# Attention, maxout and softplus layers in one kernel: turns of q a slot earlier, turns of k at the end of a batch

## The chip, the cores and the metric

The kernel runs on one core of one Trainium2 chip. The metric is the time of one execution on the device, in microseconds. TensorE does the matrix products, VectorE (DVE) and ScalarE (ACT) the work on elements, SyncE (SP) starts most of the transfers. What is measured is the median of several executions; the lines of a profile come from one profiled execution.

## The reference

The inputs are q, k, v of shape (8 batches, 8 heads, 576, 64), a short sequence p (8, 8, 32, 64), three weights of 512 x 768, one of 768 x 512, one of 512 x 2048 and one of 2048 x 512. Cut to what is computed:

```python
def sm_attn(qq, kk, vv):
    s = scale * np.matmul(qq, kk.transpose(0, 1, 3, 2))
    s = s - np.max(s, axis=-1, keepdims=True)
    a = np.exp(s)
    a = a / (np.sum(a, axis=-1, keepdims=True) + 1e-09)
    return np.matmul(a, vv)
p_packed = sm_attn(p, k, v)                  # 32 rows per head
out = sm_attn(q, p_packed, p_packed)         # 576 rows per head
x = out.transpose(0, 2, 1, 3).reshape(4608, 512)
h = np.maximum(np.maximum(x @ w1, x @ w2), x @ w3)   # layers 1
x = h @ w_out                                        # layer 2
h = x @ w_in                                         # layer 3
g = np.maximum(h, 0.0) + np.log1p(np.exp(-np.abs(h)))
y = g @ w_out2                                       # layer 4
```

The weights come as 64-bit numbers and the products are made to nearly full 32-bit precision.

## The kernel before

**Precision.** A product of two 32-bit matrices is made of three products: each operand is split into a part "hi" (`split`, ACT, L107) and a rest "lo" (DVE, L108), and hi x hi, hi x lo and lo x hi are added (`three`, L396). Names with hi and lo are such pairs: a2 (the attention weights of a batch), pw (the packed values times the first weights), h (the maxout), wi (weights of layer 3), x2 (its inputs).

**First stage, batch by batch.** A prelude with an order written out by hand does batch 0 and prepares batch 1. Then a loop over n = 1 to 7 does layer 1 and layer 2 of batch n, and between them, in small pieces, the attention of batch m = n + 1. A batch has ten slots. Slots 0 to 5 are the six blocks f of layer 1, three units w each (`layer1_unit`, unit u = 3 x slot + w). A unit is 24 matmuls; the first maxout copy `m` of a block is on ACT (L419), the two others are a maximum on DVE (L421). One slot later `layer1_split` splits the block into hhi (ACT) and hlo (DVE). Slots 6 to 9 are the four blocks e of layer 2, whose results xs leave ACT for the buffer x2d in device memory.

**The attention pieces** stand at fixed units: `attn1_scores` (p times k, needs all four turned pieces of k) at u = 5, its transposes at 9, the values at 13, `attn2_scores` (q times packed p, needs all four turned pieces of q) at 18, behind layer 1. `packed_weights`, which makes a part of pw (matmuls ps_w, L375), stands at u = 1, 5, 9, 13 and 18.

**Loads and turns.** q and k of a batch are loaded in four pieces each (`load_raw`, two heads a piece, four DMAs of 140 KB, L158, tiles qraw and kraw from one pool `rx` of four buffers). A piece is then turned, which is a transpose of 32 x 32 blocks on DVE (`transpose_kq`, L223 for k, L220 for q), into its part of the tile vT. vT has one buffer, for k and q by turns. Two lists, `loads` and `turns`, say in which slot a piece is loaded and turned, for which batch ahead.

**Narrowing.** The weights of layers 3 and 4 are 64-bit. In slots 0 to 5 `narrow_ahead` loads a block of them (L635), takes one that was loaded three steps before, makes it 32-bit with one ACT step (L79) and three DVE steps (L86, L89, L97) and stores it from the SP queue (L631, wi<-x).

**The last batch** has no attention to prepare. There the kernel loads the weights of layer 3 in 32 bits (`wi_x`, L684, four buffers), two per slot, and splits each one slot later (wihi on ACT, wilo on DVE). At the end of slot 5 it asks for the first four pieces of x2 (`x2r<-x2d`, L701), which are split in slots 7 and 8.

**What sets the order.** The pieces of TensorE's work are chained in the order of the program text (`pinned`). For DVE, ACT and SP the framework's scheduler chooses each engine's order, from the program text and its own model of when operands are there. Each engine and each queue runs its list in order, and each instruction waits for its operands.

**Second stage.** Layers 3 and 4 take 144 steps (`layer3` with the softplus, `layer4`, L782 to L784), after all batches.

Of the kernel before, what the change touches and what calls it, by code (L numbers as in the profile page):

```python
# [1 line left out]

# [17 lines left out]
def packed_attention_maxout_softplus(  # L20
# [22 lines left out]
    nc = tc.nc  # L43
# [5 lines left out]
    DF2 = wi2.shape[1] // 2  # L49
# [5 lines left out]
    KC = DM // P  # L55
    F1 = DF1 // P
# [49 lines left out]
    def split(src, hi, lo):  # L106
        nc.scalar.activation(out=hi, in_=src, func=AF.Copy)  # L107
        nc.vector.tensor_tensor(out=lo, in0=src, in1=hi.bitcast(F32), op=ALU.subtract)  # L108
# [10 lines left out]
    wsb_ctx = ExitStack()  # L119
    wsbp = wsb_ctx.enter_context(tc.tile_pool(name="wsbp", bufs=1))  # L120
    at_ctx = ExitStack()
    rx = at_ctx.enter_context(tc.tile_pool(name="rx", bufs=4, side="right"))
    vp = at_ctx.enter_context(tc.tile_pool(name="vp", bufs=1, side="right"))
    vvp = at_ctx.enter_context(tc.tile_pool(name="vvp", bufs=1, side="right"))
    ep = at_ctx.enter_context(tc.tile_pool(name="ep", bufs=2, side="right"))
# [42 lines left out]
    def load_v(n, queue=nc.sync):  # L168
        t = vvp.tile([32 * TI, H, NI, D], F32, name="vt")
        queue.dma_start(  # L170
            out=t.rearrange("p h i d -> p h (i d)"),
            in_=v[n].rearrange("h (p r) d -> p h (r d)", r=NI),
        )
        vt[n] = t
# [253 lines left out]
    def layer1_split(n, f):  # L428
        m = ms.pop((n, f)).rearrange("p h c -> p (h c)")
        hhi = hx.tile([P, S], F32R, tag="hx", name="hhi")  # L430
        hlo = hx.tile([P, S], F32R, tag="hx", name="hlo")
        split(m, hhi, hlo)
        hts[n, f] = (hhi, hlo)
# [47 lines left out]
    def narrow_w(f, w, t):  # L481
# [14 lines left out]
        PW1 S1 L10 E10 L11 Tq10 LW32 N32 PW2 E11 LO2 L1S1 L12 LW40 LW41 LW42 N40 N41  # L496
        LW50 N50 N42 PW3 LW51 N51 LW52 N52 L1S2 Vv1 PT1 SO2 L13 LO3 SO3 L14 PW4 L1S3
        L1S4 L15 PWn Lq12 Tq11 Lp2 Lq13 LO4 LO5 Tq12 SO4 SO5 Lk20 L1S0 L1S5 Lk21 Tq13 Lk22
        Lk23 A1 L20 L21 L22 L23 W10 X10 W11 X11 Tk20 Tk21
    """  # L500
    w_raw, wo_raw, steps = {}, {}, {}

# [37 lines left out]
    for name in order.split():  # L540
# [3 lines left out]
    loads = [  # L544
        (0, 1, 0, "q"),
        (0, 1, 1, "q"),
        (1, 1, 2, "q"),
        (1, 1, 3, "q"),
        (3, 2, 0, "k"),
        (4, 2, 1, "k"),  # L550
        (5, 2, 2, "k"),
        (6, 2, 3, "k"),
    ]
    turns = [
        (0, 1, 2, "k"),
        (0, 1, 3, "k"),
        (2, 1, 0, "q"),
        (3, 1, 1, "q"),
        (4, 1, 2, "q"),
        (5, 1, 3, "q"),  # L560
        (8, 2, 0, "k"),
        (9, 2, 1, "k"),
    ]
    chain = []

    def pinned(fn, *args):

        if chain:
            with tc.issue_after(chain[-1]):
                fn(*args)  # L570
        else:
            fn(*args)
        chain.append(
            next(
                i
                for i in reversed(nc.cur_bb.bb.instructions)
                if i.engine == mybir.EngineType.PE
            )
        )

    def small_work(n, u):


        m = n + 1
        more = m < B
        if u == 2 and more:
            pinned(prep_p, m)
            if m + 1 < B:
                load_p(m + 1)
        if u in (1, 5, 9, 13):  # L590
            pinned(packed_weights, n, (u + 3) // 4)
        if not more:
            return
        if u == 5:
            pinned(attn1_scores, m)
        elif u == 9:
            for G in range(NG):
                pinned(attn1_transpose, m, G)
        elif u == 13:
            pinned(attn1_values, m)  # L600
        elif u == 16:
            pinned(packed_transpose, m)
        elif u == 18:
            pinned(attn2_scores, m)
            pinned(packed_weights, m, 0)
        elif u == 20:
            for G in range(NG):
                attn2_weights(m, G)
        elif u == 21:
            for G in range(NG):  # L610
                attn2_split(m, G)

    wi_parts, wi_ready, x2 = [], [], {}
# [11 lines left out]
    def narrow_ahead():  # L625
        if len(in_flight) == AHEAD or not to_narrow and in_flight:
            raw64, dst = in_flight.pop(0)
            x = nwp.tile([P, 512], F32, tag="x32", name="x32")
            rebase(raw64, x)
            narrow(raw64, x)  # L630
            nc.sync.dma_start(out=dst, in_=x)  # L631
        if to_narrow:
            src, dst = to_narrow.pop(0)
            t = stp.tile([P, 512, 2], I32, tag="st", name="raw64")
            nc.sync.dma_start(out=t.rearrange("p n t -> p (n t)"), in_=src)  # L635
            in_flight.append((t, dst))

    for n in range(1, B):
        for slot in range(F1 + KC):

            if 1 <= slot <= F1:
                layer1_split(n, slot - 1)
            if slot < F1:
                if slot == 1 and n + 1 < B:
                    load_v(n + 1)
                for w in range(3):
                    small_work(n, 3 * slot + w)
                    pinned(layer1_unit, n, slot, w)
            else:
                small_work(n, 2 * F1 + slot)  # L650
                pinned(layer2, n, slot - F1)
            for at, ahead, g, which in turns:
                if at == slot and n + ahead < B:
                    transpose_kq(n + ahead, g, which)
            for at, ahead, g, which in loads:
                if at == slot and n + ahead < B:
                    load_raw(n + ahead, g, which)
            if 0 < n < B - 1 and slot < F1:
                narrow_ahead()
            if n + 1 == B:  # L660

                if slot == 0:
                    at_ctx.close()
                    wip = ctx.enter_context(
                        tc.tile_pool(name="wip", bufs=4, side="right", reuse_waits="tile")
                    )
                    w32p = ctx.enter_context(
                        tc.tile_pool(name="w32p", bufs=4, side="right", reuse_waits="tile")
                    )
                for c, e, x in wi_ready:  # L670
                    split(x, wi_parts[c][0][:, e], wi_parts[c][1][:, e])
                wi_ready = []
                for c, e in [divmod(2 * slot + i, KC) for i in range(2)]:
                    if c == DF2 // 512:
                        break
                    if e == 0:
                        wi_parts.append(
                            tuple(
                                wip.tile([P, KC, 512], F32R, tag=f"wi{x}", name=f"wi{x}")
                                for x in ("hi", "lo")  # L680
                            )
                        )
                    x = w32p.tile([P, 512], F32, tag="w32", name="wi_x")
                    nc.sync.dma_start(  # L684
                        out=x, in_=wi32[e * P : e * P + P, c * 512 : c * 512 + 512]
                    )
                    wi_ready.append((c, e, x))
                if slot == F1 - 1:
                    wsb_ctx.close()
                    x2p0 = ctx.enter_context(  # L690
                        tc.tile_pool(name="x2p0", bufs=KC, side="right", reuse_waits="tile")
                    )
                    xrp = ctx.enter_context(
                        tc.tile_pool(name="xrp", bufs=KC, side="right", reuse_waits="tile")
                    )

                    def load_x2(c, pool):
                        x2[c] = []
                        for e in range(KC):
                            t = xrp.tile([P, CH], F32, tag="xr", name="x2r")  # L700
                            nc.sync.dma_start(  # L701
                                out=t,
                                in_=x2d[e * P : e * P + P, c * CH : c * CH + CH],
                            )
                            hi = pool.tile([P, CH], F32R, tag="x2hi", name="x2hi")
                            lo = pool.tile([P, CH], F32R, tag="x2lo", name="x2lo")
                            x2[c].append((t, hi, lo))

                    load_x2(0, x2p0)
                if slot in (F1 + 1, F1 + 2):  # L710
                    for e in range(KC // 2):
                        split(*x2[0][(slot - F1 - 1) * (KC // 2) + e])
    aps_ctx.close()
    a_ctx.close()

# [90 lines left out]
    for i in range(len(seq) + SKEW):  # L806
        if 1 <= i <= len(seq):
            split_g(*seq[i - 1])
        if i < len(seq):
            c, f = seq[i]  # L810
# [48 lines left out]
```

## Time and profile before

| | us |
|---|---|
| median of 3 executions (lowest, highest) | 1389.2 (1387.06, 1391.03) |
| profiled execution | 1388.84 |
| its span, first to last instruction | 1387.0 |
| TensorE busy | 1317.1 |
| DVE busy, ACT busy | 896.3, 619.4 |
| first layer 2 starts | 105.49 |
| layer 3 starts | 582.17 |

A line of the time line has the start, the length, the engine, the line of the kernel, the operation, the tiles written and read, and in square brackets the idle time ahead of it with what ended it. SPq is the SP queue; the length of a row of several DMAs there is the time in which they were issued, not the time until they landed. A line of the waits has the waiting instruction, what it waited for, the total, the count and the longest. The granted clock is TensorE's, as a share of full speed.

### The profile page before, as it was taken

Reading aid. Unit: us, or ns where it says so; the run is one execution under the profiler, and the core shown is the slowest. Engines: PE = TensorE matmul, PEld = TensorE weight load, DVE = VectorE, ACT = ScalarE, POOL = GpSimd, SP = SyncE. Lnnn points to the kernel's source line nnn. Section 1 sums busy time; section 2 is a strip of 40 time slices with the busy share of each in tenths; the row PEclk is TensorE's granted clock in tenths of the full one; section 3 lists DMA queues with packets and bytes.
Section 4 is the critical chain, followed back from the end, with each engine's and each line's share of the span. In section 5 each row is a group of like instructions: output and inputs, shape, how many; then the busy total and the mean of one; then the engine's idle time right before and its main releaser. Section 6 shows DMA issues by size and latency. Waiting matters only on the chain.

```text
span 1387.0 us, 21473 instructions
## 1 busy us (share of the span) xinstructions
PE 1317.1 (95%) x8656; PEld 1105.2 (80%) x8656; DVE 896.3 (65%) x1480; ACT 619.4 (45%) x1045; POOL 0.7 (0%) x6
## 2 busy tenths in 40 slices
PE   4889999898989899899999999999999999999998
PEld 3668888787878788878888888888888888888886
DVE  4787877676767665585656556566565665655654
ACT  3443443334343334564545445454454544544443
POOL 0000000000000000000000000000000000000000
PEclk9999999999999999999999999999999999999999
DMA  9774775848474721620201102011020010000101
GB/s 276 191 210 122 187 180 145 215 116 207 138 200 149 211 64 52 219 85 1 61 1 31 31 0 61 1 31 31 0 61 0 15 47 1 18 14 0 31 1 31
DMA packets 61861, 119.18 MB, mean 86 GB/s; under 512 B 11073, under 2 KB 28737, under 8 KB 61761
## 3 DMA queue, kind: packets, MB, share of 16 engines
q1 hardware_dynamic: 55984, 106.66, 28.9%
q10 hardware_dynamic: 5776, 11.14, 2.4%
q8 instruction: 68, 1.11, 0.3%
q14 instruction: 33, 0.26, 0.1%
HBM read 90.51 MB, written 27.26 MB: 85 GB/s over the span
## 4 chain that ended last, share of the span: by engine, by line
PE 88%; DMA 4%; DVE 4%; issue 1%; ACT 1%; SPq 1%; DVEq 0%
PE ps L396 54%; PE acc L783 9%; PE acc L784 9%; PE acc L782 9%; PE ps_w L375 2%; PE ps_s L247 1%; DMA qraw<-in_q_dram 1%; PE ps_e L286 1%; DMA wraw<-in_moe_w_dram 1%; DMA wi_x<-wi 1%; PE ps_v L306 1%; DVE m L421 0%; DVE pwlo L108 0%; DMA woraw<-in_moe_w_out_dram 0%; DMA kraw<-in_k_dram 0%
## 5 line engine op out<-in xcount | busy, mean ns | idle before, releaser
L396 PE MATMUL ps<-x2hi,wilo 128*128 128x512 f32 x576 | 228.0, 396 | 0.0
L396 PE MATMUL ps<-x2hi,wihi 128*128 128x512 f32 x576 | 226.8, 394 | 0.7 <-ACT xs L453 0.7
L396 PE MATMUL ps<-x2lo,wihi 128*128 128x512 f32 x576 | 227.0, 394 | 0.0
L783 PE MATMUL acc<-w2lo,ghi 128*128 128x512 f32 x576 | 225.7, 392 | 0.0
L784 PE MATMUL acc<-w2hi,glo 128*128 128x512 f32 x576 | 225.4, 392 | 0.0
L782 PE MATMUL acc<-w2hi,ghi 128*128 128x512 f32 x576 | 224.5, 390 | 0.8 <-ACT ghi L107 0.8
L107 ACT ACTIVATE ghi<-t 128x512 fp32r<-128x512 f32 x144 | 91.1, 632 | 292.5 <-DVE t L763 292.1
L756 DVE TENSOR_SCALAR t<-ex 128x512 f32<-128x512 f32 x144 | 61.4, 426 | 164.2 <-ACT ex L753 164.2
L108 DVE TENSOR_TENSOR glo<-t,ghi 128x512 fp32r<-128x512 f32 x144 | 99.7, 692 | 92.8 <-ACT ghi L107 92.7
L396 PE MATMUL ps<-a2hi,pwhi 128*128 128x288 f32 x576 | 131.3, 311 | 2.4 <-ACT a2hi L107 1.3
L782 PEld LDWEIGHTS acc<-w2hi,ghi 128*128 128x128 f32 x576 | 108.2, 188 | 25.9 <-ACT ghi L107 1.2
L396 PEld LDWEIGHTS ps<-x2lo,wihi 128*128 128x128 f32 x576 | 108.1, 188 | 25.8
L396 PEld LDWEIGHTS ps<-x2hi,wihi 128*128 128x128 f32 x576 | 108.1, 188 | 25.5 <-ACT xs L453 1.0
L396 PEld LDWEIGHTS ps<-x2hi,wilo 128*128 128x128 f32 x576 | 108.3, 188 | 25.2
L783 PEld LDWEIGHTS acc<-w2lo,ghi 128*128 128x128 f32 x576 | 108.1, 188 | 25.1
L752 ACT ACTIVATE ex<-ps 128x512 f32<-128x512 f32 x144 | 86.2, 598 | 91.8 <-PE ps L396 91.8
L784 PEld LDWEIGHTS acc<-w2hi,glo 128*128 128x128 f32 x576 | 108.1, 188 | 23.1
L396 PE MATMUL ps<-a2lo,pwhi 128*128 128x288 f32 x576 | 125.8, 301 | 0.7 <-DVE a2lo L108 0.7
L396 PE MATMUL ps<-a2hi,pwlo 128*128 128x288 f32 x576 | 125.6, 300 | 0.0
L759 DVE TENSOR_TENSOR t<-ln,t 128x512 f32<-128x512 f32 x144 | 99.7, 692 | 30.5 <-ACT ln L754 30.5
L421 DVE TENSOR_TENSOR m<-ps,m 128x576 f32<-128x576 f32 x96 | 72.5, 756 | 57.5 <-PE ps L396 56.1
L396 PEld LDWEIGHTS ps<-a2hi,pwhi 128*128 128x128 f32 x576 | 95.0, 196 | 17.1 <-issue 6.5
(90 smaller groups left out, 1891.7 us busy)
## 6 DMA issues: line engine op xcount, KB each, us to landing
qraw<-in_q_dram SPq DMA_DIRECT2D x112, 140.0 KB
kraw<-in_k_dram SPq DMA_DIRECT2D x96, 140.0 KB
wraw<-in_moe_w_dram SPq DMA_DIRECT2D x18, 512.0 KB
x2d<-xs ACTq DMA_DIRECT2D x32, 288.0 KB
x2r<-x2d SPq DMA_DIRECT2D x36, 256.0 KB
out_dram<-o SPq DMA_DIRECT2D x136, 64.0 KB
raw<-in_moe_w_in_dram SPq DMA_DIRECT2D x16, 512.0 KB
raw<-in_moe_w_out_dram SPq DMA_DIRECT2D x16, 512.0 KB
```

Of the source, the lines that this page charges most:

```text
L107: nc.scalar.activation(out=hi, in_=src, func=AF.Copy)
L108: nc.vector.tensor_tensor(out=lo, in0=src, in1=hi.bitcast(F32), op=ALU.subtract)
L247: nc.tensor.matmul(ps[G][cols, hh, :HS], w[rows, cols], x[rows, g, hh * HS : hh * HS + HS], start=True, stop=True,)
L375: nc.tensor.matmul(ps[cols, G, : units * P].rearrange("p (w x) -> p w x", w=units), ppT[n][rows, cols], wsb[rows, 4 * c : 4 * c + units, g ...
L396: nc.tensor.matmul(o, w, xx, start=first, stop=last)
L421: nc.vector.tensor_tensor(out=m, in0=ps[:, :, :HS], in1=ms[n, f], op=ALU.max)
L752: nc.scalar.activation(out=ex, in_=ps, func=AF.Abs)
L756: nc.vector.tensor_scalar(out=t, in0=ex, scalar1=1.0, scalar2=-1.0, op0=ALU.add, op1=ALU.add)
L759: nc.vector.tensor_tensor(out=t, in0=ln, in1=t, op=ALU.subtract)
L782: nc.tensor.matmul(ps, ghi[:, cols], whi, start=(f == 0), stop=False)
L783: nc.tensor.matmul(ps, ghi[:, cols], wlo, start=False, stop=False)
L784: nc.tensor.matmul(ps, glo[:, cols], whi, start=False, stop=(f == F2 - 1))
```

## The change

Three things change. The turns of q move from slots 2 to 5 to slots 1 to 4. The turns of k, which had been two in slots 8 and 9 of one batch and two in slot 0 of the next, are all in slot 9 (the last two of batch 2 are in the prelude now). The loads move with them, and the pool of raw pieces has five buffers in place of four. In the last batch the splits of layer-3 weights of slots 6 to 9 may not be issued before the ACT part of the block's maxout split (`tc.issue_after`), the weights are asked for by a table (none in slot 4, two more in slot 8), and the splits of x2 move from slots 7 and 8 to 6 and 7.

```diff
-    rx = at_ctx.enter_context(tc.tile_pool(name="rx", bufs=4, side="right"))
+    rx = at_ctx.enter_context(tc.tile_pool(name="rx", bufs=5, side="right"))
...
-        Lk23 A1 L20 L21 L22 L23 W10 X10 W11 X11 Tk20 Tk21
+        Lk23 A1 L20 L21 L22 L23 W10 X10 W11 X11 Tk20 Tk21 Tk22 Tk23
...
     loads = [
         (0, 1, 0, "q"),
         (0, 1, 1, "q"),
-        (1, 1, 2, "q"),
+        (0, 1, 2, "q"),
         (1, 1, 3, "q"),
-        (3, 2, 0, "k"),
-        (4, 2, 1, "k"),
-        (5, 2, 2, "k"),
-        (6, 2, 3, "k"),
+        (4, 2, 0, "k"),
+        (5, 2, 1, "k"),
+        (6, 2, 2, "k"),
+        (7, 2, 3, "k"),
     ]
     turns = [
-        (0, 1, 2, "k"),
-        (0, 1, 3, "k"),
-        (2, 1, 0, "q"),
-        (3, 1, 1, "q"),
-        (4, 1, 2, "q"),
-        (5, 1, 3, "q"),
-        (8, 2, 0, "k"),
+        (1, 1, 0, "q"),
+        (2, 1, 1, "q"),
+        (3, 1, 2, "q"),
+        (4, 1, 3, "q"),
+        (9, 2, 0, "k"),
         (9, 2, 1, "k"),
+        (9, 2, 2, "k"),
+        (9, 2, 3, "k"),
     ]
...
             if 1 <= slot <= F1:
                 layer1_split(n, slot - 1)
+                l1_done = last_of(mybir.EngineType.Activation)
...
-                for c, e, x in wi_ready:
-                    split(x, wi_parts[c][0][:, e], wi_parts[c][1][:, e])
+                with tc.issue_after(l1_done) if slot >= F1 else nullcontext():
+                    for c, e, x in wi_ready:
+                        split(x, wi_parts[c][0][:, e], wi_parts[c][1][:, e])
+                    if slot in (F1, F1 + 1):
+                        for e in range(KC // 2):
+                            split(*x2[0][(slot - F1) * (KC // 2) + e])
                 wi_ready = []
-                for c, e in [divmod(2 * slot + i, KC) for i in range(2)]:
-                    if c == DF2 // 512:
-                        break
+                lot = {0: 0, 1: 2, 2: 4, 3: 6, 5: 8, 6: 10, 7: 12, 8: 14}.get(slot)
+                for c, e in [divmod(lot + i, KC) for i in range(2)] if lot is not None else ():
...
-                if slot in (F1 + 1, F1 + 2):
-                    for e in range(KC // 2):
-                        split(*x2[0][(slot - F1 - 1) * (KC // 2) + e])
```

The entries of `loads` and `turns` are (slot, batches ahead, piece, which). F1 is 6.

The order of TensorE's instructions is the same in both programs. Three places show how the others move. First DVE around `attn1_scores` of a batch in the middle, where the last turn of k (L223) and the first maxima of the scores (L262) are. Before:

```order
L108 TENSOR_TENSOR pwlo<-ps_w,pwhi 128x512
L421 TENSOR_TENSOR m<-ps_3072,m 128x576
L223 STREAM_TRANSPOSE vT<-kraw 128x6x3x32
L108 TENSOR_TENSOR hlo<-m,hhi 128x576
L421 TENSOR_TENSOR m<-ps_3128,m 128x576
L86 TENSOR_SCALAR raw_2777<-x_3274 128x512
L89 SCALAR_TENSOR_TENSOR raw_2777<-raw_2777 128x512
L97 SCALAR_TENSOR_TENSOR x_3274<-x_3274,raw_2777 128x512
L108 TENSOR_TENSOR pwlo<-ps_w,pwhi 128x512 x2
L223 STREAM_TRANSPOSE vT<-kraw 128x6x3x32
L262 TENSOR_REDUCE mx<-ps_s 128x1 x2
```

And after the change, at the same place:

```order
L97 SCALAR_TENSOR_TENSOR x_3275<-x_3275,raw_2772 128x512
L108 TENSOR_TENSOR pwlo<-ps_w,pwhi 128x512
L223 STREAM_TRANSPOSE vT<-kraw 128x6x3x32
L108 TENSOR_TENSOR pwlo<-ps_w,pwhi 128x512
L421 TENSOR_TENSOR m<-ps_3052,m 128x576
L421 TENSOR_TENSOR m<-ps_3074,m 128x576
L108 TENSOR_TENSOR hlo<-m,hhi 128x576
L421 TENSOR_TENSOR m<-ps_3133,m 128x576
L223 STREAM_TRANSPOSE vT<-kraw 128x6x3x32
L108 TENSOR_TENSOR pwlo<-ps_w,pwhi 128x512 x2
L262 TENSOR_REDUCE mx<-ps_s 128x1 x2
```

The last turn of k stood behind a narrowing (L86, L89, L97) and two pwlo; now it stands directly behind the maximum, and that narrowing comes before the units.

Second, DVE at the end of layer 1 of the same batch, around the last turn of q (L220) and the first step of the second softmax (L333). Before:

```order
L421 TENSOR_TENSOR m<-ps_2683,m 128x576
L220 STREAM_TRANSPOSE vT<-qraw 128x576
L108 TENSOR_TENSOR hlo<-m,hhi 128x576
L421 TENSOR_TENSOR m<-ps_2735,m 128x576
L421 TENSOR_TENSOR m<-ps_2750,m 128x576
L108 TENSOR_TENSOR hlo<-m,hhi 128x576
L220 STREAM_TRANSPOSE vT<-qraw 128x576
L333 STREAM_TRANSPOSE s_2801<-ps_s 128x576
```

And after the change:

```order
L421 TENSOR_TENSOR m<-ps_2679,m 128x576
L220 STREAM_TRANSPOSE vT<-qraw 128x576
L108 TENSOR_TENSOR hlo<-m,hhi 128x576
L86 TENSOR_SCALAR raw_2419<-x_2700 128x512
L421 TENSOR_TENSOR m<-ps_2731,m 128x576
L89 SCALAR_TENSOR_TENSOR raw_2419<-raw_2419 128x512
L421 TENSOR_TENSOR m<-ps_2746,m 128x576
L97 SCALAR_TENSOR_TENSOR x_2700<-x_2700,raw_2419 128x512
L86 TENSOR_SCALAR raw_2477<-x_2766 128x512
L108 TENSOR_TENSOR hlo<-m,hhi 128x576
L89 SCALAR_TENSOR_TENSOR raw_2477<-raw_2477 128x512
L333 STREAM_TRANSPOSE s_2796<-ps_s 128x576
```

The turn that stands here was the third piece of q and is now the fourth, the last; around the last two maxima there are now pieces of a narrowing that stood behind L333 before.

Third, ACT in the last batch, from the last packed weights (pwhi, 128x256) to the last block of layer 1 (its first unit's copy is m<-ps_6556 before and m<-ps_6550 after). Before:

```order
L107 ACTIVATE wihi<-wi_x 128x512 x4
L107 ACTIVATE pwhi<-ps_w 128x256
L107 ACTIVATE x2hi<-x2r 128x512 x2
L107 ACTIVATE pwhi<-ps_w 128x256
L107 ACTIVATE wihi<-wi_x 128x512 x3
L419 ACTIVATE m<-ps_6556 128x576
L107 ACTIVATE wihi<-wi_x 128x512
L107 ACTIVATE hhi<-m 128x576
L107 ACTIVATE x2hi<-x2r 128x512 x2
L107 ACTIVATE wihi<-wi_x 128x512 x3
L107 ACTIVATE hhi<-m 128x576
```

And after the change:

```order
L107 ACTIVATE pwhi<-ps_w 128x256 x2
L107 ACTIVATE wihi<-wi_x 128x512 x3
L107 ACTIVATE hhi<-m 128x576
L107 ACTIVATE wihi<-wi_x 128x512
L419 ACTIVATE m<-ps_6550 128x576
L107 ACTIVATE wihi<-wi_x 128x512 x3
L107 ACTIVATE hhi<-m 128x576
L107 ACTIVATE wihi<-wi_x 128x512
L107 ACTIVATE x2hi<-x2r 128x512 x2
```

The two pwhi come first now, the splits of x2 come behind both hhi, and seven splits of weights are ahead of the last hhi where there were eleven. On the SP queue of the last batch four loads of wi_x stand ahead of the first x2r, before and after. The second of them now waits for the last ps_w of TensorE, whose memory it reuses since the fifth raw buffer shifted the tiles; the third and fourth stand behind it in the queue.

More of the change, by code (lines that the diff above doesn't have):

```diff
@@ L1 @@
-from contextlib import ExitStack
+from contextlib import ExitStack, nullcontext
 import concourse.bass as bass
@@ L546, in packed_attention_maxout_softplus, with last_of @@
         (0, 1, 1, "q"),
-        (1, 1, 2, "q"),
+        (0, 1, 2, "q"),
         (1, 1, 3, "q"),
-        (3, 2, 0, "k"),
-        (4, 2, 1, "k"),
-        (5, 2, 2, "k"),
-        (6, 2, 3, "k"),
+        (4, 2, 0, "k"),
+        (5, 2, 1, "k"),
+        (6, 2, 2, "k"),
+        (7, 2, 3, "k"),
     ]
     turns = [
-        (0, 1, 2, "k"),
-        (0, 1, 3, "k"),
-        (2, 1, 0, "q"),
-        (3, 1, 1, "q"),
-        (4, 1, 2, "q"),
-        (5, 1, 3, "q"),
-        (8, 2, 0, "k"),
+        (1, 1, 0, "q"),
[3 more added lines that the diff above has]
+        (9, 2, 0, "k"),
         (9, 2, 1, "k"),
+        (9, 2, 2, "k"),
+        (9, 2, 3, "k"),
     ]
     chain = []
+    def last_of(engine):
+        return next(i for i in reversed(nc.cur_bb.bb.instructions) if i.engine == engine)
     def pinned(fn, *args):
@@ L572, in pinned @@
             fn(*args)
[L573 to L579, printed above, removed]
+        chain.append(last_of(mybir.EngineType.PE))
     def small_work(n, u):
```

## The prediction

> **What bounds the kernel now.** I read the busy shares first, then the windows by batch, then the waits of TensorE, and last the time lines around the longest of them. The page says that one engine carries the time:
>
> ```profile
> span 1387.0 us, 21473 instructions
> PE 1317.1 (95%) x8656; PEld 1105.2 (80%) x8656; DVE 896.3 (65%) x1480; ACT 619.4 (45%) x1045; POOL 0.7 (0%) x6
> ```
>
> TensorE is idle for 69.9 us of 1387.0, so a change that moves turns and loads and keeps every matmul can win at most that, and what low clock the idling causes. The windows below run from one start of layer 2 to the next (layer 2 of one batch, layer 1 of the next one, attention for the one after; span, PE busy, PEld, DVE, ACT, POOL, then the granted clock, the DMA share and GB/s):
>
> ```profile
> 105.49:165.53 60.04, 59.23 (x622) 53.07 (x614) 45.11 (x80) 23.97 (x43) 0.00 (x0) 1.00 0.55 146
> 165.53:227.80 62.27, 59.52 (x623) 53.24 (x615) 45.43 (x79) 24.03 (x43) 0.00 (x0) 1.00 0.70 181
> 227.80:297.74 69.94, 63.51 (x617) 55.25 (x615) 48.45 (x85) 25.31 (x44) 0.00 (x0) 0.94 0.66 169
> 297.74:367.14 69.40, 62.96 (x616) 55.19 (x615) 47.78 (x83) 24.98 (x44) 0.00 (x0) 0.94 0.65 170
> 367.14:434.84 67.70, 61.26 (x617) 53.92 (x615) 46.76 (x82) 24.98 (x44) 0.00 (x0) 0.97 0.64 175
> 434.84:504.17 69.33, 62.89 (x617) 54.69 (x615) 48.32 (x85) 25.31 (x44) 0.00 (x0) 0.95 0.49 138
> 504.17:582.17 78.00, 74.09 (x571) 69.58 (x569) 41.77 (x68) 32.27 (x55) 0.00 (x0) 0.98 0.39 125
> ```
>
> The same work of a batch (615 weight loads) takes 60.04 us in the first row and 67.70 to 69.94 in four others. The last row ends with layer 2 of the last batch, where layer 3 starts, and has no attention left. What the slow rows hold is in the waits of TensorE (total us, times, longest):
>
> ```profile
> PE ps_s L247 <- DVE vT L223: 16.1, 4, 4.0
> PE ps_s L247 <- DVE vT L220: 12.1, 5, 2.4
> ...
> PE ps L396 <- ACT hhi L107: 1.6, 1, 1.6
> PE ps L396 <- ACT m L419: 1.3, 1, 1.3
> ```
>
> L223 is the turn of k, L220 that of q: four waits of 4.0 us and five of 2.4, in the five batches whose rows are long. The two small waits stand in the last batch. Everything from 582 us on is layers 3 and 4, 144 steps that the change does not touch.
>
> **The wait for k.** Around the first one, TensorE and then VectorE:
>
> ```profile
> 257.37 0.68 PE L247 MATMUL ps_s<-vT,pT 64*32 64x288 f32 x12
> 262.07 1.22 PE L247 MATMUL ps_s<-vT,pT 64*32 64x288 f32 x16 [4.02 <-DVE vT L223]
> ```
> ```profile
> 256.67 0.76 DVE L421 TENSOR_TENSOR m<-ps,m 128x576 f32<-128x576 f32 x1 [1.00 <-PE ps L396]
> 257.34 0.42 DVE L86 TENSOR_SCALAR raw<-x 128x512 int32<-128x512 int32 x1
> ...
> 258.52 0.69 DVE L97 SCALAR_TENSOR_TENSOR x<-x,raw 128x512 int32<-128x512 int32 x1
> ...
> 260.48 0.69 DVE L108 TENSOR_TENSOR pwlo<-ps_w,pwhi 128x512 fp32r<-128x512 f32 x1 [0.66 <-ACT pwhi L107]
> 261.08 0.93 DVE L223 STREAM_TRANSPOSE vT<-kraw 128x576 f32<-128x576 f32 x1
> ```
>
> The scores of turns k0 to k2 run (twelve matmuls), then TensorE stands from 258.05 until the last turn ends at 262.01. That turn is queued on VectorE behind a narrowing (L86, L89, L97) and two pwlo. Its data is late too, since k3's four loads are the last of the queue:
>
> ```profile
> 232.22 9.50 SPq L158 DMA_DIRECT2D kraw<-in_k_dram  x4
> 246.22 8.19 SPq L158 DMA_DIRECT2D kraw<-in_k_dram  x4
> ...
> 255.75 3.66 SPq L158 DMA_DIRECT2D qraw<-in_q_dram  x8
> ...
> 260.98 10.46 SPq L158 DMA_DIRECT2D qraw<-in_q_dram  x8
> ```
>
> After the change all four turns of k belong to the end of the batch before. The order shows the last of them directly behind the maxout at 256.67, with the narrowing before that one. By these rows it starts at 257.34 in place of 261.08 and ends at 258.27, against 258.05 when TensorE wants it. So 0.2 to 0.4 us of the 4.02 remain, 1.2 at most over four batches. The data allows it: k2 and k3 are now eight issues in a row behind the second narrowed store, where k2 alone went out at 232.22. With the two longest groups seen, 9.50 and 8.19, they are all issued by 250, and the turn is wanted at 257.3. The fifth raw buffer is what lets k3 be loaded before a turn frees one.
>
> **The wait for q.** The second kind:
>
> ```profile
> 294.79 0.92 PE L247 MATMUL ps_s<-vT,ppT 64*32 64x288 f32 x18 [2.41 <-DVE vT L220]
> ```
> ```profile
> 288.41 0.76 DVE L108 TENSOR_TENSOR hlo<-m,hhi 128x576 fp32r<-128x576 f32 x1
> ...
> 291.79 0.76 DVE L421 TENSOR_TENSOR m<-ps,m 128x576 f32<-128x576 f32 x1 [0.77 <-PE ps L396]
> 293.29 0.76 DVE L108 TENSOR_TENSOR hlo<-m,hhi 128x576 fp32r<-128x576 f32 x1 [0.75 <-ACT hhi L107]
> 293.97 0.77 DVE L220 STREAM_TRANSPOSE vT<-qraw 128x576 f32<-128x576 f32 x1
> ```
>
> The last turn of q stands behind the last maxout and the last hlo of the batch, while TensorE wants it at 292.38. After the change it stands two maxouts and two hlo earlier, ahead of the hlo at 288.41, some 5.5 us before its old place. Its loads: before, they were issued by 271.4 (260.98 plus 10.46), 22.5 us ahead of the turn. Now twelve of the sixteen follow p at once, and the last four follow behind a store and two loads. I cost this wait at nothing left; what hides it are those 22.5 us, of which an earlier turn uses 5 and a later issue perhaps 5 more. Were the cover gone, the 2.41 would be back per batch.
>
> What VectorE does in place of the turn, around the last hlo, are the narrowing pieces of two weight tiles. L86 to L97 are 0.42 and twice 0.69, so an hlo can be late by one piece. I take 0 to 0.7 us per batch, five times, and book 1 us in all: VectorE stands idle 0.77 us ahead of the maxout and 0.75 ahead of the hlo in these rows, room for a piece each.
>
> **What the idle time costs beside itself.** The clock behind the waits:
>
> ```profile
> 225.85:233.00 7.15, 7.15 (x75) 1.00 0.13 41
> 262.07:268.90 6.83, 6.83 (x42) 0.54 1.10 262
> 294.79:299.20 4.41, 4.41 (x42) 0.61 0.02 4
> 558.08:564.67 6.59, 4.78 (x32) 1.00 0.71 237
> 564.67:569.00 4.33, 4.28 (x20) 0.61 0.68 157
> ```
>
> These are stretches right behind waits: q at 225.85, k at 262.07, q at 294.79, and the last batch (behind m, then behind hlo). The k wait is followed by 6.83 us at a clock of 0.54, a loss of 6.83 x 0.46 = 3.1 us. The q wait loses nothing in one batch and 4.41 x 0.39 = 1.7 in the other. So the waits are dearer than their idle time. Summed over the four slow batches by their mean clocks, the loss is 63.51 x 0.06 + 62.96 x 0.06 + 61.26 x 0.03 + 62.89 x 0.05 = 12.6 us.
>
> **The sum for the batches, two ways.** By waits: 16.1 + 12.1 + 12.6 = 40.8 us. By intervals: the five long rows exceed 60.04 by 2.23 + 9.90 + 9.36 + 7.66 + 9.29 = 38.4; the first row has 0.8 us of small waits of its own. I take 40. Less 1.2 for what is left of k and 1 for the narrowing pieces, that is 37.8.
>
> **The last batch.** Here ACT is the engine to look at:
>
> ```profile
> 548.69 2.20 ACT L107 ACTIVATE wihi<-wi_x 128x512 fp32r<-128x512 f32 x4
> ...
> 556.18 1.30 ACT L107 ACTIVATE wihi<-wi_x 128x512 fp32r<-128x512 f32 x2 [0.69 <-DMA wi_x<-wi]
> 557.39 0.63 ACT L419 ACTIVATE m<-ps 128x576 f32<-128x576 f32 x1
> ```
> ```profile
> 550.68 5.48 DMA wi_x<-wi
> ...
> 558.83 3.78 DMA wi_x<-wi
> ```
>
> The maxout at 557.39 waits behind weight splits that wait for their loads; TensorE stops 1.3 us for it, then 1.6 for hhi, and then runs 4.33 us at 0.61. That is 1.3 + 1.6 + 1.7 = 4.6 us to be had. The change puts splits behind the part of the maxout on ACT, but not behind all: from slot 6 on they follow the slot's own layer-1 split, and three of them still stand ahead of the hhi of the fifth unit, three ahead of that of the sixth. Their loads also change place. Before, four were in SBUF; now only the first needs no wait, and three leave the SP queue once ps_w is done, at 548.7. At 3.78 to 5.48 us a load they land at 552.5 to 554.2, two splits and an hhi later (1.30 + 0.68) it is 554.5 to 556.2, and the maxout can follow one more split later, at 555.1 to 556.8. TensorE wants it at 556.8 (558.08 less 1.32). The next three splits hang on loads issued 2 to 4 us later by the same rows, so their hhi comes 0 to 1.5 us late. I take a loss of 1 in this place, gain 3.5; its bounds are a gain of 4.6 and a loss of 5.5 (one whole load not hidden).
>
> A page of the Trainium skill bears on the size of this term. "TensorE: Matmul & The Clock Gate", Part 1, says the clock drops only after an idle window of some 3.4 us. By that rule the last batch's waits of 1.3 and 1.6 us would cost no clock, the term would be 1.7 smaller and the time some 1349 us. The trace disagrees here, with 0.61 behind short waits, at 294.79 behind 2.41 us of idling as well; at 225.85 it agrees, with 1.00.
>
> The profiled run took 1388.84 us, 1.84 around its span of 1387.0, and the median of the runs is 1389.2, 0.4 more. 1388.84 - 37.8 - 3.5 = 1347.5 by this run; with the 0.4 about 1348. The count by waits is the more direct of the two and is 0.8 above the 40 that I took: I say **1347 us**.
>
> **The rivals.**
> *One of the two waits stays.* A turn can stand early and its data still be late. If k stays, only q goes: 12.1 and three clock losses of 1.7, 17.2, with the 3.5 that is 1368.5. If q stays: 40.8 - 17.2 = 23.6 for k, 1362. For it: k3's loads did arrive late, 8.19 us of issuing. Against it: 7 us in hand for k, over 10 for q.
> *The last batch gets worse.* SP now holds three weight loads behind ps_w which were in SBUF before. If ACT stops a whole load (5.48) before hhi with a clock loss as behind k (3.1), and the old 4.6 go, the batch ends 4 us later than before: 1389.2 - 37.8 + 4 = 1355. For it, ACT takes its list in order, as the split at 556.18 shows; against it, three splits now stand ahead of hhi and not four.
> *Slower: the queue.* Eight loads of k, two of p and twelve of q now leave SP as one block. If every group of four took the 9.50 us of the longest one, six groups take 57 us from 234 on, to 291, and with 4 to landing and the turn q3 is there at 296, where it is wanted at 292.4; the block would slip further each batch, by some 4 us. Slower than before it is from the point where the new wait passes 40.8 / 5 = 8 us per batch; at 12 us it is 20 us more, 1410. Against it: eight loads took 3.66 us at 255.75, and the DMA share of these windows is 0.49 to 0.70.
> *No change.* A scheduler could put the turns back where the data lands. Against it, the order shows them moved. 1388.
>
> **How the numbers follow.** Forecast 0.76, one wait stays 0.07, worse last batch 0.10, the queue 0.04, no change 0.03. The likeliest case's own range is 1342 (all 40.8 + 4.6, and 2 of small waits) to 1356 (38.4 less 1.2 of k and 3.5 of narrowing, nothing of the last batch). To hold 8 in 10 I reach to the worse last batch: 1340 to 1358. A measurement tells 0.3%, some 4 us, from no change. Faster is 0.76 + 0.07 + 0.10 = 0.93 and 0.01 of the case of no change, 0.94; same 0.02; slower 0.04.
>
> **What would show it.** Right: the waits on L223 and L220 gone from TensorE's list but for some tenths, the seven windows from layer 2 to layer 2 all at 59.5 to 60.5 with a clock of 1.00, layer 3 starting near 541. Wrong in the k step: a wait on the turn of k over 1 us. Wrong in the last batch: an interval there not under 76. A new wait of hlo, a2lo or pwlo on each batch would mean that the narrowing pieces cost more than the 1 us. The forecast as a whole fails if q3 or k3 lands after its turn is reached.

## The result: 1340.7 us, and the profile after

The changed kernel takes 1340.71 us (median of 4, 1338.59 to 1342.63) against 1390.12 us for the one before on the same chip. The ratio is 0.9647, 95% interval 0.9624 to 0.967: 49 us or 3.5% faster. The forecast was 1347 with a range of 1340 to 1358; the time lies 0.7 us above the range's low end.

The profiled execution of the changed kernel took 1342.63 us, the slowest of its four. Its page begins:

```profile
span 1340.8 us, 21459 instructions
PE 1299.9 (97%) x8656; PEld 1096.9 (82%) x8656; DVE 894.9 (67%) x1480; ACT 618.6 (46%) x1045; POOL 0.7 (0%) x6
```

TensorE's idle time fell from 69.9 to 40.9 us. Its busy time fell as well, by 17.2 us at the same number of matmuls: they ran less often at a low clock. The windows from layer 2 to layer 2, in the columns of the prediction:

```profile
107.57:167.70 60.13, 59.33 (x623) 53.10 (x615) 45.44 (x81) 24.56 (x44) 0.00 (x0) 1.00 0.50 136
167.70:226.89 59.19, 58.87 (x623) 53.02 (x615) 45.77 (x81) 24.51 (x44) 0.00 (x0) 1.00 0.72 191
226.89:286.27 59.38, 59.07 (x623) 53.08 (x615) 47.13 (x83) 24.98 (x45) 0.00 (x0) 1.00 0.76 200
...
405.01:464.38 59.37, 59.06 (x623) 53.07 (x615) 46.94 (x82) 24.03 (x43) 0.00 (x0) 1.00 0.60 171
464.38:536.01 71.63, 71.63 (x576) 68.06 (x569) 42.53 (x67) 31.24 (x53) 0.00 (x0) 1.00 0.38 125
```

The first interval is as long as before. The five batches that had been long take 59.2 to 59.4 us at full clock, and the last interval is 71.63 us without any idle time. Stretch by stretch, for the two profiled executions:

| stretch | before | after | difference |
|---|---|---|---|
| up to the first layer 2 | 105.49 | 107.57 | +2.1 |
| first interval | 60.04 | 60.13 | +0.1 |
| five batches | 338.64 | 296.68 | -42.0 |
| last interval, to layer 3 | 78.00 | 71.63 | -6.4 |
| layers 3 and 4, to the end of the span | 804.8 | 804.8 | 0.0 |

Of the waits on turns, TensorE's list still has one row:

```profile
PE ps_s L247 <- DVE vT L223: 1.2, 4, 0.3
```

No row for L220 is left. The place where it had stood 4.02 us for k, on TensorE, on VectorE and on the SP queue:

```profile
256.43 0.68 PE L247 MATMUL ps_s<-vT,pT 64*32 64x288 f32 x12
257.42 0.92 PE L247 MATMUL ps_s<-vT,pT 64*32 64x288 f32 x18 [0.31 <-DVE vT L223]
```
```profile
255.72 0.76 DVE L421 TENSOR_TENSOR m<-ps,m 128x576 f32<-128x576 f32 x1 [0.90 <-PE ps L396]
256.40 0.97 DVE L223 STREAM_TRANSPOSE vT<-kraw 128x576 f32<-128x576 f32 x1
```
```profile
234.05 11.08 SPq L158 DMA_DIRECT2D kraw<-in_k_dram  x8
...
257.78 2.49 SPq L158 DMA_DIRECT2D qraw<-in_q_dram  x4
```

The last turn of k starts as the maximum ends and is 0.31 us late. Its data was asked for by 245.1, and that of the last piece of q by 260.3. At the end of layer 1, the last turn of q ends at 281.47, 2.8 us before TensorE starts the matmuls that need it. Before the change TensorE had waited 2.41 us for it:

```profile
280.70 0.77 DVE L220 STREAM_TRANSPOSE vT<-qraw 128x576 f32<-128x576 f32 x1
```
```profile
284.28 1.20 PE L247 MATMUL ps_s<-vT,ppT 64*32 64x288 f32 x32
```

### The profile page after: what moved, and what is told of

It is laid out like the page before. It is cut to its first block, busy times and chain, and to the rows that moved or that the text cites. A ratio compares the mean times of both kernels' runs of the same rounds, so it can differ in the third digit from the quotient of the medians.

```text
span 1340.8 us, 21459 instructions
## 1 busy us (share of the span) xinstructions
PE 1299.9 (97%) x8656; PEld 1096.9 (82%) x8656; DVE 894.9 (67%) x1480; ACT 618.6 (46%) x1045; POOL 0.7 (0%) x6
## 4 chain that ended last, share of the span: by engine, by line
PE 92%; DMA 3%; DVE 3%; ACT 1%; issue 1%; SPq 0%; DVEq 0%
PE ps L396 57%; PE acc L781 10%; PE acc L782 10%; PE acc L780 10%; PE ps_w L375 2%; DMA wraw<-in_moe_w_dram 1%; PE ps_s L247 1%; PE ps_e L286 1%; DMA kraw<-in_k_dram 1%; PE ps_v L306 1%; DMA vt<-in_v_dram 1%; PE ps_k L199 1%; DVE pwlo L108 0%; DMA w_x<-wo 0%; DVE wraw L89 0%
## 5 line engine op out<-in xcount | busy, mean ns | idle before, releaser
L761 DVE SCALAR_TENSOR_TENSOR t<-ps,t 128x512 f32<-128x512 f32 x144 | 99.5, 691 | 4.7
```

The source lines that it names most:

```text
L761: nc.vector.scalar_tensor_tensor(out=t, in0=ps, scalar=0.0, in1=t, op0=ALU.max, op1=ALU.add)
```

## The experiments: which edit did it

The change has four parts: the turns and loads of q, those of k, the fifth raw buffer, and the edits in the last batch. Theory 1, by which the prediction reckoned, says that each part removes its own wait. Theory 2 says that only the place of the two last turns on VectorE matters, and that a small shift moves both. The first runs take one part at a time.

**The q part alone** (four buffers):

```diff
     loads = [
         (0, 1, 0, "q"),
         (0, 1, 1, "q"),
-        (1, 1, 2, "q"),
+        (0, 1, 2, "q"),
         (1, 1, 3, "q"),
     turns = [
         (0, 1, 2, "k"),
         (0, 1, 3, "k"),
-        (2, 1, 0, "q"),
-        (3, 1, 1, "q"),
-        (4, 1, 2, "q"),
-        (5, 1, 3, "q"),
+        (1, 1, 0, "q"),
+        (2, 1, 1, "q"),
+        (3, 1, 2, "q"),
+        (4, 1, 3, "q"),
```

> Only the q part of the change: q2 loaded in slot 0, the turns of q in slots 1 to 4; k, four raw buffers and the last batch as before. Theory 1, each edit removes its own wait: the waits on L220 go, those on L223 (16.1 us) stay; 12.1 us and some clock, about 1373 us. Theory 2, what decides is the place of the last k turn on DVE, and the narrowing that stood ahead of it moves with any shift of the program: in this kernel's order the last k turn already stands directly behind the maximum, so the waits on L223 should fall to some tenths too, the five long intervals to about 59.4, and the time to 1348 to 1350.

Measured: 1346.14 us, ratio 0.9673 (0.965 to 0.9696). Its waits, and one batch and the last interval (span, PE busy, clock, DMA share, GB/s):

```profile
PE ps_s L247 <- DVE vT L223: 1.2, 4, 0.3
```
```profile
285.69:345.07 59.38, 59.08 (x623) 1.00 0.73 199
...
463.80:539.33 75.53, 72.40 (x577) 1.00 0.40 129
```

Theory 2 holds: without an edit to k, the waits for k are gone too. Each batch is as short as in the whole change. Only the last interval is longer, by 3.9 us.

**The k part alone**, with its fifth buffer:

```diff
-    rx = at_ctx.enter_context(tc.tile_pool(name="rx", bufs=4, side="right"))
+    rx = at_ctx.enter_context(tc.tile_pool(name="rx", bufs=5, side="right"))
...
-        (3, 2, 0, "k"),
-        (4, 2, 1, "k"),
-        (5, 2, 2, "k"),
-        (6, 2, 3, "k"),
+        (4, 2, 0, "k"),
+        (5, 2, 1, "k"),
+        (6, 2, 2, "k"),
+        (7, 2, 3, "k"),
...
-        (0, 1, 2, "k"),
-        (0, 1, 3, "k"),
...
-        (8, 2, 0, "k"),
+        (9, 2, 0, "k"),
         (9, 2, 1, "k"),
+        (9, 2, 2, "k"),
+        (9, 2, 3, "k"),
```

> Only the k part: all four turns of k in slot 9, its loads one slot later, five raw buffers; q and the last batch as before. Theory 1, each edit its own wait: L223 goes, L220 stays (12.1 us), 1362 to 1366 us. Theory 2, the place decides: in this kernel's order the last k turn still stands behind two pwlo (2 x 0.68 us), so 1.5 to 1.8 us of each wait of 4.0 stay, 6 to 7 us over four batches, and the L220 waits too; 1370 to 1378.

Measured: 1381.09 us, ratio 0.9928 (0.9906 to 0.995), slower than both theories said. The waits, and VectorE around one of them:

```profile
PE ps_s L247 <- DVE vT L223: 12.9, 4, 3.2
PE ps_s L247 <- DVE vT L220: 12.1, 5, 2.4
```
```profile
260.64 0.73 DVE L421 TENSOR_TENSOR m<-ps,m 128x576 f32<-128x576 f32 x1
262.24 0.69 DVE L108 TENSOR_TENSOR pwlo<-ps_w,pwhi 128x512 fp32r<-128x512 f32 x1 [0.87 <-ACT pwhi L107]
263.59 0.69 DVE L108 TENSOR_TENSOR pwlo<-ps_w,pwhi 128x512 fp32r<-128x512 f32 x1 [0.66 <-ACT pwhi L107]
264.20 0.93 DVE L223 STREAM_TRANSPOSE vT<-kraw 128x576 f32<-128x576 f32 x1
```

With all four turns of k at the end of the batch in the program's text, the last one still stands behind both pwlo, and those wait for ACT (0.87 and 0.66 us). My figure of 1.5 to 1.8 us counted only their work, 2 x 0.69, and left out their waits. It also shows what the narrowing was worth in the kernel before: its three steps ran largely while VectorE would have waited for ACT, so taking them away gains 0.8 us of 4.02. The five batches gain 3.8 us here (62.94 + 66.26 + 68.24 + 68.75 + 68.61 = 334.8), and the last interval, 71.91, gains 6.1.

**Which number of the q part?** One run has only the load of q2 moved (first diff), one only the four turns (second diff); both keep four buffers.

```diff
-        (1, 1, 2, "q"),
+        (0, 1, 2, "q"),
```
```diff
-        (2, 1, 0, "q"),
-        (3, 1, 1, "q"),
-        (4, 1, 2, "q"),
-        (5, 1, 3, "q"),
+        (1, 1, 0, "q"),
+        (2, 1, 1, "q"),
+        (3, 1, 2, "q"),
+        (4, 1, 3, "q"),
```

> Only the load of q2 in slot 0, one number; four raw buffers, all turns as before. Theory 2: as the q part alone, batches at 59.4, last interval 75.5, 1343 to 1347. Theory 1: no wait goes, 1389.

> Only the turns of q in slots 1 to 4, their loads as before, four raw buffers. This is the edit that the words of the change begin with. Theory 2: the order of DVE hardly differs from before, the last turns of k and q stand where they stood, so the waits of 16 and 12 us stay: 1387 to 1392. Theory 1: the waits on L220 go, about 1373.

Measured, in one execution each: 1347.13 us with the load, 1388.04 us with the turns. A batch and the waits, first of the load, then of the turns:

```profile
287.12:346.50 59.38, 59.07 (x622) 1.00 0.77 199
```
```profile
PE ps_s L247 <- DVE vT L223: 1.2, 4, 0.3
```
```profile
294.37:363.53 69.16, 62.73 (x617) 0.95 0.62 171
```
```profile
PE ps_s L247 <- DVE vT L223: 16.1, 4, 4.0
PE ps_s L247 <- DVE vT L220: 12.1, 5, 2.4
```

Moving the turns in the text does nothing: in that kernel's order the last turn of q stands behind the last hlo and the last of k behind the narrowing and two pwlo, just as before. Moving the load of one piece by one slot gives the order of the changed kernel at both places. That is the order as built.

The moved load also takes k's loads forward on the SP queue. The four of k3 are issued by 246.0, where they had been issued by 254.4:

```profile
234.87 11.11 SPq L158 DMA_DIRECT2D kraw<-in_k_dram  x4
```

So this run alone does not part the place of the turn from the time of its data. In the kernel before, the turn starts right behind the pwlo without idle time (the rows of the prediction), so there its place held it. The runs with a held turn, further down, keep the early data and bring the wait back. Whether the old loads would have been in time for the new place isn't shown. Why the scheduler answers to the load and not to the turn wasn't tried; that it places a turn by when its own model has the data there would fit.

**The last batch.** Its edits alone, on the kernel before (four buffers), and the whole change without them:

> Only the part in the last batch (splits behind the maxout, the table of loads, the splits of x2 a slot earlier); turns, loads and four raw buffers as before. Theory 1, the last batch gains by itself what the whole change gained there, 6.4 us (71.63 against 78.00 from layer 2 of batch 6 to layer 3): 1383 to 1384. Rival: 1.5 to 3 us of it belong to the q wait that ran into the clock of this stretch or to the fifth buffer, and it gains the 3.5 of the prediction: 1386 to 1387.

> The changed kernel without the part in the last batch: k and q parts and five raw buffers, last batch as before. If the parts add up: 1390.1 less 42.0 for the batches plus 2.1 for a later start of the first layer 2, 1348 to 1350, the last interval at 76 to 78. Rival: the fifth buffer makes three weight loads wait for the last ps_w, and with the old order of splits that stops TensorE more than before: last interval 79 to 82, 1351 to 1354.

Measured: 1387.43 us (0.9975, 0.9955 to 0.9994) and 1340.83 us (0.9639, 0.9616 to 0.9663). The last intervals, of the edits alone and then of the change without them:

```profile
505.95:579.81 73.86, 72.32 (x570) 1.00 0.41 132
```
```profile
461.18:532.83 71.65, 71.65 (x576) 1.00 0.40 129
```

The edits alone gain 4.1 of the 6.4 us. In the whole change they gain nothing: 71.65 without, 71.63 with them, and both expectations for the run without them were wrong. So the fifth buffer was tried by itself:

```diff
-    rx = at_ctx.enter_context(tc.tile_pool(name="rx", bufs=4, side="right"))
+    rx = at_ctx.enter_context(tc.tile_pool(name="rx", bufs=5, side="right"))
```

> Only five raw buffers in place of four. If the fifth buffer alone does the last batch (three of its weight loads then wait for the last ps_w, and the scheduler puts the two pwhi and an hhi ahead of their splits): last interval 71.7 to 72 in place of 78.0, the batches unchanged, 1390 - 6 = 1384. If the edits of the last batch were needed for it: interval 77 to 78, 1389 to 1391.

Measured: 1385.92 us, 0.9962 (0.9949 to 0.9976). Its last interval, and ACT there:

```profile
507.91:580.21 72.30, 72.30 (x571) 0.99 0.40 128
```
```profile
552.97 0.38 ACT L107 ACTIVATE pwhi<-ps_w 128x256 fp32r<-128x256 f32 x1
...
554.12 0.62 ACT L107 ACTIVATE wihi<-wi_x 128x512 fp32r<-128x512 f32 x1
556.44 1.31 ACT L107 ACTIVATE wihi<-wi_x 128x512 fp32r<-128x512 f32 x2 [1.69 <-DMA wi_x<-wi]
557.66 0.67 ACT L107 ACTIVATE hhi<-m 128x576 fp32r<-128x576 f32 x1
558.23 0.61 ACT L107 ACTIVATE wihi<-wi_x 128x512 fp32r<-128x512 f32 x1
558.75 0.63 ACT L419 ACTIVATE m<-ps 128x576 f32<-128x576 f32 x1
```

The fifth buffer takes all the idle time out of this interval (span and busy time are both 72.30) without any edit to the splits: 5.7 of the 6.4 us, and the other 0.7 is clock, behind a q wait that this kernel still has. It shifts memory so that three weight loads wait for TensorE's last ps_w, which looks like a loss. But the order then has the two pwhi first, and the hhi of the fifth block ahead of the fourth split, and the copy for the maximum at 558.75 is in time. TensorE, which had waited 1.3 us for that copy, waits for nothing here. That the buffer works by this order is read from the rows; no run has five buffers and the old order.

**The smallest version.** If theory 2 is all, two numbers are enough: the load of q2 in slot 0, and five buffers.

> The kernel before with two numbers changed: the load of q2 in slot 0 (was 1), and five raw buffers. No turn is moved, k's loads and the last batch are as before. Theory 2 (the place of the last turns on DVE is all that matters, and this load alone moves them; the fifth buffer does the last batch): batches at 59.4, last interval 71.7, no waits on L220, 1.2 us on L223: the same as the whole change, 1339 to 1343 us. Theory 1 (the turns' slots and the last batch's edits carry the gain): 1370 or more.

Measured: 1341.92 us, 0.9651 (0.9624 to 0.9677), which the measurement can't tell from the whole change. Its batches are the same, and its last interval is 0.9 us longer, most of it a wait of 0.7 us for xs that the whole change doesn't have:

```profile
285.78:345.16 59.38, 59.06 (x622) 1.00 0.78 199
...
463.92:536.45 72.53, 71.79 (x577) 1.00 0.41 134
```

**What a wait costs.** The change gained 42.0 us in five batches, where the waits fell by 27.0 (28.2 to 1.2). The other 15.0 are busy time of TensorE, and 13.3 of them are clock: the stretches at half clock in these batches before hold 26.7 us of work. Four runs put a wait of a chosen length into four batches, the last run into six: the turn of k3 is held back by multiplications of its piece by 1, in place, one, two, four and five of them, and in the last run the turn is also moved to unit 5. The third run's edit:

```diff
+                    if (which, g) == ("k", 3):
+                        held = raw[n + ahead, g, "k"].rearrange("p t b d -> p (t b d)")[:, :512]
+                        for _ in range(4):
+                            nc.vector.tensor_scalar(
+                                out=held, in0=held, scalar1=1.0, scalar2=None, op0=ALU.mult
+                            )
                     transpose_kq(n + ahead, g, which)
```

> The changed kernel with one idle multiplication by 1 (0.43 us on DVE, in place) ahead of the last turn of k, which stands behind the maximum as before: the wait on L223 grows from 0.3 to 0.7 us a batch. Theory a, a wait costs itself: intervals 59.8. Theory b, every wait on this spot costs half as much again in clock (as 28.2 us of waits cost 42.0): 59.9 to 60.0, hardly to be told apart here; it is the low end of the curve.

> The same with two multiplications, and a pwlo falls between them and the turn: a wait of 1.5 to 2.2 us a batch. Theory a: intervals 59.1 plus the wait, 60.6 to 61.3, clock 1.00. Theory b: 59.1 plus 1.5 times the wait, 61.4 to 62.4, with stretches at half clock behind some of the waits.

> Four multiplications, among them two pwlo, ahead of the turn: a wait of 3 to 4 us a batch. Theory a: 62.1 to 63.1. Theory b: 63.6 to 65.1. With a drop of the clock behind each wait, as in the kernel before (4.02 us, then 6.83 us at 0.54), a batch costs the wait and 3 us.

> The last turn of k held back to unit 5, behind two pwlo and five multiplications: a wait of 5 to 6 us a batch. Theory a: 64.1 to 65.1. Theory b: 66.6 to 68.1. If the loss of clock is one stretch of fixed length whatever the wait, 59.1 plus the wait plus 1.7 or 3: 66 to 68.

Times of one execution each: 1343.91, 1349.41, 1361.97 and 1385.72 us. Two batches of the first three, in this order, and three of the last:

```profile
225.71:285.52 59.81, 59.06 (x623) 1.00 0.75 198
285.52:345.68 60.16, 59.06 (x622) 1.00 0.75 197
```
```profile
286.89:349.34 62.45, 60.57 (x622) 0.97 0.71 189
349.34:410.28 60.94, 59.06 (x623) 1.00 0.69 194
```
```profile
226.49:291.41 64.92, 61.67 (x622) 0.95 0.69 183
...
421.18:483.49 62.31, 59.06 (x622) 1.00 0.61 163
```
```profile
306.53:373.56 67.03, 61.51 (x622) 0.95 0.66 177
373.56:439.63 66.07, 60.56 (x622) 0.97 0.65 179
```

The busy time tells the clock's part, since the matmuls are the same: 59.06 us is a batch at full clock. A wait of 0.7 us (1.1 in one batch) costs itself. One of 1.9 us costs itself in three batches, and in one batch 1.5 us more. One of 3.25 us costs 2.6 us more in three batches, and in the fourth nothing more. One of 5.5 us costs 1.5 to 2.5 more in all six, as the last expectation had it for one stretch of low clock whatever the wait. So neither theory a nor theory b holds: a wait costs itself and, if it is long, often a loss of 1.5 to 2.6 us, which doesn't grow with the wait. The same wait at the same place of the same kernel can go either way, in the windows of the third run ahead of and behind two waits:

```profile
256.71:259.96 3.25, 0.00 (x1) 0.83 0.87 219
259.96:268.00 8.04, 8.04 (x52) 0.64 1.06 235
451.40:454.65 3.25, 0.00 (x1) 1.00 1.07 316
454.65:463.00 8.35, 8.35 (x84) 1.00 1.09 215
```

The granted clock in the traces tells the two apart. It is 1.00 or 0.50 and nothing else, and from the first layer 2 to layer 3 each stretch at 0.50 lasts 3.41 or 6.83 us. They begin on a raster, a fixed grid in time, of 3.413 us: in the kernel before at 261.55, 295.68, 333.23 and 363.95, which are 10, 11 and 9 periods apart. The periods of that raster around the same two waits:

```profile
255.44:258.85 3.41, 1.27 (x28) 1.00 0.94 219
258.85:265.68 6.83, 5.72 (x35) 0.50 1.02 245
...
449.99:453.40 3.41, 1.41 (x28) 1.00 1.02 323
453.40:456.81 3.41, 2.16 (x28) 1.00 1.10 216
```

The first wait leaves TensorE idle for 0.63 of a period, the other for 0.59 of one and 0.37 of the next. From 107 to 580 us of all the profiles, each of the 50 drops follows a period that was idle for 0.54 to 1.00 of its length, and of the periods without a drop behind them none was idle for more than 0.59. So in these profiles the idle share of one period decides, and with it how a wait falls on the raster. Where the raster lies differs from execution to execution.

The Trainium skill, "TensorE: Matmul & The Clock Gate", Part 1, describes a free-running window of about 3.4 us in which activity is watched. That equal waits come out differently, by where they fall on a raster of 3.413 us, agrees with a free-running window. That the clock should drop only after an idle window of some 3.4 us does not agree: it dropped behind 1.9 and 3.25 us.

## Why the prediction was right, and where not

*The bound and the waits.* Right: the time was in the waits on the two last turns and in the clock behind them, and both went.

*What is left of k.* Said 0.2 to 0.4 us a batch, 1.2 in four; measured 0.31, and 1.2. The loads of k2 and k3, said to be issued by 250, were issued by 245.1. The fifth buffer, which the prediction held to be what lets k3 come early, isn't needed for it: with four buffers and the load of q2 moved, the wait is the same.

*What is left of q.* Said nothing; measured nothing. The loads, thought to be issued perhaps 5 us later, were issued 11 us earlier (by 260.3 and not 271.4).

*The narrowing pieces.* I booked 1 us; no new wait on hlo, pwlo or a2lo stands in the five batches, where one of 0.2 us on pwlo is all there is. The pieces went into VectorE's idle time ahead of the last maxout and the last hlo (0.77 and 0.75 us before).

*The sum for the batches.* Said 37.8, measured 42.0. Of the 4.2 us, 2.4 are the clock term: I booked 12.6, and TensorE's busy time in the five batches fell by 15.0 (310.1 to 295.1), 13.3 of it clock and 1.7 that the granted clock doesn't account for. Another 1.0 is the narrowing that cost nothing, and 0.8 is the choice of 40 in place of the 40.8 by waits. What drew me below 40.8 was the way by intervals: it took 60.04 us, the first row, for a clean batch. That interval keeps its 60.1 us after the change and is longer than the others for reasons of its own; a clean batch is 59.3. Five times 0.7 is 3.5, and with it the 38.4 would have been 41.9. So the sign that I named, windows of 59.5 to 60.5, was too high as well.

*The last batch.* Said a gain of 3.5 with a bound of 4.6; measured 6.4. The bound was too low. I counted two waits (1.3 and 1.6) and one stretch of low clock (1.7). The window before had 78.00 - 74.09 = 3.9 us idle, 1.0 of it small waits on hlo and xs that I left out, and 74.09 - 71.63 = 2.5 us more of busy time. Of that, 1.7 is the clock that I counted. The other 0.8 isn't clock: the run with the q part alone still has its two long waits there and is busy for 72.40 us at a clock of 1.00. The cause was wrong too: I took the fifth buffer's wait of three loads for a cost, and the order of splits for the gain. Alone, the buffer takes away the waits, and with it the edits give nothing.

*Layer 3 from 541 us on.* It started at 536.0, by these two terms, less 2.1 us in the prelude, which I had not thought of. The windows of 0 to 102.9 us, of the change and then of the change without its last-batch edits, whose prelude is built in the same order:

```profile
0.00:102.90 102.90, 71.20 (x881) 0.82 0.88 227
```
```profile
0.00:102.90 102.90, 74.69 (x908) 0.93 0.88 228
```

The same prelude reached its first layer 2 at 107.57 in one execution and at 104.52 in the other, with more of it at a low clock in the first. So this is a difference between executions and not one that the last-batch edits make, and the kernel before lies between them at 105.49. Most of the 4 us by which the four times of the changed kernel differ may be there. The time is 6 us below the forecast because the two terms together were 7 us too small. That it still lies in the range, by 0.7 us, is partly luck: one of the four executions, at 1338.59, is below it.

*The rivals.* "One of the two waits stays", "the last batch gets worse" and "slower: the queue" did not come; the loads from k2 to q3 were issued in 26 us (234.05 to 260.27), not in 57. "No change" was given 0.03 and its mechanism is real: the scheduler put the turns back where they had been, as the run with the turns alone shows. The loads saved the change. I argued from the order of the whole program and did not ask which edit had made it.

## What to carry to other kernels

Where a scheduler orders an engine's instructions, ask of each edit what it does to the built order, alone: here turns moved in the text moved nothing, and one load moved by one slot gave the 42 us. Price a wait of about 2 us or more on TensorE as itself plus a possible loss of clock of about 2 us, and take the clean length of a loop from its busy time at full clock, not from the shortest interval that the profile happens to show. A step that is late by its queue can be mended by what stands ahead of it, and what stands ahead counts with its own waits.

## What was not expected of the hardware

Two things, both above: equal waits of 3.25 us at the same place of a batch were followed by a stretch at 0.64 of the clock in one batch and by 1.00 in another, by how they fell on a raster of 3.413 us, and a wait of 1.9 us was enough once in four. And the prelude, where TensorE waits for its first data, differs by some 3 us between executions of the same order.
